# Attention with beacons and a max-out FFN on one core: the steps of the first two batches in another order

## The chip, the core and the metric

The kernel runs on one core of a Trainium2 chip. The core has five engines that run side by side and wait for each other through semaphores: TensorE (PE, matrix products and transposes; its weight loads are shown apart as PEld), VectorE (DVE), ScalarE (ACT), GpSimd (POOL) and SyncE (SP, which here only issues transfers). Sixteen DMA engines move data between the device's memory and the on-chip memory; a request for a transfer stands in the queue of the engine that issues it (SP, ACT or POOL), in that engine's order. The metric is the device time of one execution in microseconds (us).

## What is computed

```python
def _attn_ref(q, k, v, beacon_k, beacon_v):          # B, H, S, Nb, D = 8, 8, 576, 16, 64
    scale = 1.0 / np.sqrt(D)
    k_all = np.concatenate([beacon_k, k], axis=2)
    v_all = np.concatenate([beacon_v, v], axis=2)
    scores = scale * np.matmul(q, k_all.transpose(0, 1, 3, 2))
    causal[:, Nb:] = np.triu(np.ones((S, S), dtype=bool), k=1)
    scores = np.where(causal, -1000000000.0, scores)
    scores = scores - scores.max(-1, keepdims=True)
    a = np.exp(scores)
    a /= a.sum(-1, keepdims=True) + 1e-09
    return np.matmul(a, v_all)

def _moe_ref(x, w1, w2, w3, w_out):                  # x: 4608 x 512, w: 512 x 768, w_out: 768 x 512
    h = np.maximum(np.maximum(x @ w1, x @ w2), x @ w3)
    return h @ w_out
```

All inputs and the output are float32. The heads' attention results of a token, side by side, are a row of x.

## The kernel before

The eight heads of a batch are worked on as four pairs (p is the pair's number over all batches, four to a batch), and two pairs make a quad. For each pair the kernel needs qT and kT, that is q and k with the head dimension on the partitions. In batches 0 to 3 PE turns them (transposes into PSUM, `turn_half` L431, `turn` L387) and another engine copies them out; six buffers of qT and kT go round (L145). In batch 0 a pair is turned in halves of 288 tokens: pair 0 and pair 1 each from their own loads (`load_half` L210, cast to bf16 by `cast_half` L218), the others from quads that a POOL transfer casts on its way (`load_quad` L226). In batch 1 a whole pair is turned at once (`load_whole_quad` L235). Later pairs are loaded in float32 (`load_pair` L192) and cast by an engine (`cast_pair` L254).

The scores of a pair stand in four groups gi (`emit_scores` L506): key tiles by ranges of queries, for both heads. PE writes a group into one of two PSUM tiles named sc (a third, named wide, is added by the step "widen"), and ACT takes the exponential into the pair's SBUF tile at_sb (L532). A mask then zeroes what lies above the diagonal, on POOL (`affine_select`, L551) or on DVE (a product with the triangle tri, L549). "values" (`emit_pv` L571) multiplies a quad's at_sb with ones (the sums) and with v; "invert" (L606) has ACT make the reciprocals, and "multiply" (L618) has DVE write the scaled result into xT, the FFN's input. The v tiles come in float32 and are cast by an engine (`load_first_v` L286, `cast_first_v` L310 in batch 0).

The FFN works on blocks of 512 tokens. Block 0 is cut into 18 half units of 256 tokens (`mm1_halves` L666): for each of the three weights, three units of 8 products each for the low half (kind 0) and three for the high half (kind 1), nine of a kind, weights in order; DVE copies or takes the maximum into hT (L681, L683). Then come units with w_out (`mm2_unit` L685, L690). The weights are fetched by POOL transfers that cast to bf16, two requests for each of the three (`load_w` L323) and one for w_out (`load_w_out` L330).

Nothing schedules this: every engine carries out its instructions in the order in which the program emits them. For batches 0 and 1 that order is a list of named steps, `first_steps` (L892), carried out one after the other (L1100). A step emits instructions on several engines at once. For example ("scores", p, gi, n) emits on PE n filler products (`spare` L479, 128x320 of a constant tile, into the tile that the scores will use) and the scores, and on ACT the exponential. ("half", p, h, bank, engine, idle, idle_q) emits idle_q pairs of small filler transposes (`fill` L407), the turn of q, idle pairs, the turn of k, a copy of q by the named engine and a copy of k by DVE. ("busy", n) emits n fillers. ("keys", p, engine) copies the beacons' keys to kT. Steps whose name begins with "load" only emit requests; where one names an engine, that engine first writes one element of the destination, and the request and all that stands behind it in its queue wait for this. After the list a loop over quads 4 to 15 (L1140 and on) goes on with the later batches, the first of it being one last half unit and the scores of pair 8. The loop is not changed.

```python
    def emit_all():
        for name, *args in first_steps:
            steps[name](*args)
```

Of the kernel before, what the change touches and what calls it, by code (L numbers as in the profile page):

```python
# [16 lines left out]
def kernel(  # L17
# [120 lines left out]
    busy = const.tile([128, 320], BF16, name="busy")  # L138
# [709 lines left out]
    def widen():  # L848
# [43 lines left out]
    first_steps = [  # L892
        ("load half", 0, 0, "sp"),
        ("busy", 17),
        ("identity",),
        ("busy", 8),
        ("triangle",),
        ("load quad half", 1, 0),
        ("load half", 1, 0, "act"),
        ("load half", 0, 1, "act"),  # L900
        ("cast half", 0, 1, "dve"),
        ("load keys 0", "act"),
        ("cast keys 0", "act"),
        ("load half", 1, 1, "sp"),
        ("cast half", 0, 0, "act"),
        ("cast half", 1, 0, "act"),
        ("load v0", 0, "dve"),
        ("half", 0, 0, "ffn", "act", 0, 7),
        ("cast half", 1, 1, "act"),
        ("turn keys 0",),  # L910
        ("load v0", 1, "pool"),
        ("keys", 3, "act"),
        ("load v0", 2),
        ("keys", 1, "act"),
        ("keys", 2, "pool"),
        ("load quad half", 0, 1),
        ("half", 1, 0, "ffn", "act", 2, 9),
        ("scores", 0, 0, 0),
        ("scores", 1, 0, 3),
        ("load w", 0),  # L920
        ("cast v0", 0, "pool"),
        ("half", 3, 0, "ffn", "act", 0, 0),
        ("mask", 0, 0, "dve"),
        ("cast v0", 1, "dve"),
        ("half", 2, 0, "pv", "dve", 4, 0),
        ("cast v0", 2, "act"),
        ("scores", 3, 0, 3),
        ("mask", 1, 0, "pool"),
        ("scores", 2, 0, 6),
        ("values", 0, 0, "pv", 0, 4, 0),  # L930
        ("half", 0, 1, "ffn", "act", 0, 7),
        ("invert",),
        ("load v0", 3, "dve"),
        ("scores", 0, 2, 4),
        ("mask", 3, 0, "dve"),
        ("mask", 2, 0, "dve"),
        ("scores", 0, 3, 0),
        ("multiply",),
        ("values", 1, 0, "ffn", 0, 4, 0),
        ("invert",),  # L940
        ("half", 1, 1, "pv", "act", 0, 0),
        ("multiply",),
        ("scores", 0, 1, 0),
        ("mask", 0, 3, "dve"),
        ("load quad half", 1, 1),
        ("scores", 1, 2, 0),
        ("load keys 1",),
        ("load v0", 4, "dve"),
        ("mask", 0, 1, "pool"),
        ("ffn", "ffn", 0),  # L950
        ("load w", 1),
        ("mask", 1, 2, "dve"),
        ("ffn", "ffn", 0),
        ("mask", 0, 2, "pool"),
        ("scores", 1, 3, 0),
        ("half", 2, 1, "pv", "act", 0, 0),
        ("scores", 1, 1, 0),
        ("ffn", "ffn", 0),
        ("mask", 1, 3, "pool"),
        ("half", 3, 1, "pv", "dve", 0, 0),  # L960
        ("scores", 2, 3, 0),
        ("cast v0", 3),
        ("load quad", 1, 0),
        ("scores", 2, 2, 7),
        ("cast v0", 4),
        ("scores", 3, 2, 0),
        ("mask", 1, 1, "dve"),
        ("cast keys 1", "pool"),
        ("values", 0, 1, "pv", 0, 4, 0),
        ("scores", 3, 3, 0),  # L970
        ("load w", 2),
        ("turn keys 1",),
        ("keys", 4, "act"),
        ("ffn", "ffn", 0),
        ("mask", 3, 3, "pool"),
        ("load v", 1, 0, "pool"),
        ("mask", 2, 3, "pool"),
        ("invert",),
        ("keys", 5, "act"),
        ("scores", 2, 1, 0),  # L980
        ("mask", 2, 2, "pool"),
        ("multiply",),
        ("ffn", "ffn", 0),
        ("mask", 2, 1, "pool"),
        ("mask", 3, 2, "pool"),
        ("ffn", "ffn", 0),
        ("scores", 3, 1, 1),
        ("mask", 3, 1, "dve"),
        ("whole", 4, "ffn", "dve"),
        ("widen",),  # L990
        ("values", 1, 1, "pv", 0, 4, 0),
        ("invert",),
        ("scores", 4, 1, 0),
        ("multiply",),
        ("scores", 4, 2, 1),
        ("whole", 5, "ring", "act"),
        ("ffn", "ring", 1),
        ("mask", 4, 1, "dve"),
        ("ffn", "ring", 1),
        ("scores", 5, 0, 1),  # L1000
        ("scores", 4, 0, 0),
        ("scores", 4, 3, 0),
        ("ffn", "pv", 1),
        ("ffn", "ring", 0),
        ("load pair", 8, "dve"),
        ("ffn", "pv", 1),
        ("scores", 5, 3, 0),
        ("mask", 5, 0, "dve"),
        ("mask", 4, 2, "dve"),
        ("mask", 5, 3, "dve"),  # L1010
        ("load pair", 9, "pool"),
        ("scores", 5, 2, 0),
        ("load quad", 1, 1),
        ("mask", 4, 3, "dve"),
        ("keys", 7, "act"),
        ("scores", 5, 1, 0),
        ("mask", 4, 0, "pool"),
        ("ffn", "pv", 0),
        ("ffn", "ring", 0),
        ("load v", 1, 1),  # L1020
        ("load", 2, "dve"),
        ("whole", 6, "ring", "dve"),
        ("keys", 6, "pool"),
        ("ffn", "pv", 1),
        ("mask", 5, 2, "pool"),
        ("cast v", 1, 0),
        ("scores", 6, 2, 0),
        ("scores", 6, 1, 0),
        ("mask", 5, 1, "pool"),
        ("scores", 6, 0, 0),  # L1030
        ("ffn", "pv", 1),
        ("load", 1),
        ("values", 2, 0, "ring", 0, 4, 0),
        ("invert",),
        ("keys", 9, "act"),
        ("cast pair", 8),
        ("load w_out", "dve"),
        ("whole", 7, "ring"),
        ("mask", 6, 0, "pool"),
        ("ffn", "pv", 1),  # L1040
        ("multiply",),
        ("cast pair", 9),
        ("load", 2, "dve"),
        ("scores", 6, 3, 0),
        ("scores", 7, 2, 0),
# [188 lines left out]
```

## Time and profile before

| | us |
|---|---|
| median of 3 runs | 294.38 (293.03 to 295.4) |
| profiled execution | 294.65 |
| its span | 292.6 |
| PE, PEld busy | 281.3 (96%), 160.1 (55%) |
| DVE, ACT, POOL busy | 169.6 (58%), 150.5 (51%), 115.8 (40%) |

The profile is that of one execution. The span begins before the first instruction and ends with the last; 2.05 us of the execution lie outside it. Times in the profile count from the span's start. PE is busy nearly throughout, but that includes the fillers, and the ends of its matmuls are modelled. What the profile offers beside totals is used below: the timeline (instructions in order, like ones merged), the chain of waits (followed back from the end), the list of who waited for whom, and busy times in windows.

The part of the program that the list makes up takes about the first 58 us. Up to there PE waits as follows (total, times, longest):

| PE operation | waited for | us |
|---|---|---|
| fillers at the start | DVE, constant tile | 1.3 |
| w_out units | DMA of w_out | 0.7 |
| scores | POOL, L551 (see the prediction) | 0.6 |
| half units | DMA of w | 0.6 |
| scores | DVE copy of qT | 0.6 |
| scores | ACT copies of qT | 0.5 and 0.3 |
| values | DVE mask | 0.4 |
| half units | DVE, xT | 0.3 |

### The profile page before, as it was taken

The page shows a single profiled execution, that of the slowest core. Times are in us where ns is not written, and L with a number is a line of the kernel's source. Part 1 is how long each engine was busy: PE and PEld are TensorE (multiplying, and loading weights), DVE is VectorE, ACT ScalarE, POOL GpSimd, SP SyncE. Part 2 cuts the span into 40 slices and gives each one's busy share as a digit, 9 for nine tenths or more (in the row PEclk, how much of TensorE's full clock was granted, in tenths as well). Part 3 has the DMA queues.
Part 4 walks back from the last instruction along what each step waited for, and adds up shares of the span by engine and source line. Part 5 has one row for each costly group of instructions (what it writes and reads, how often), then busy time and mean ns, then how long its engine had stood idle before and what let it go on. Part 6 is the DMA issues. An engine that isn't in the chain of part 4 may idle for free.

```text
span 292.6 us, 8864 instructions
## 1 busy us (share of the span) xinstructions
PE 281.3 (96%) x3714; PEld 160.1 (55%) x3739; DVE 169.6 (58%) x319; ACT 150.5 (51%) x242; POOL 115.8 (40%) x238
## 2 busy tenths in 40 slices
PE   8889999989999999999999999999999999999995
PEld 4656677754454555454545887545454545444442
DVE  1555567837756575566655656565656564474273
ACT  3786576853566676846676256635663552200300
POOL 3618415742546583426454655466323420000000
PEclk9999999999999999999999999999999999999999
DMA  7999979999989999998999899999442003001103
GB/s 131 161 175 185 217 123 225 228 192 261 229 230 256 232 281 270 186 175 263 314 190 181 233 256 268 177 205 214 104 68 98 2 0 137 11 0 74 71 1 143
DMA packets 85111, 49.50 MB, mean 169 GB/s; under 512 B 64208, under 2 KB 79824, under 8 KB 85072
## 3 DMA queue, kind: packets, MB, share of 16 engines
q1 hardware_dynamic: 78864, 43.40, 66.6%
q0 software_dynamic: 5648, 5.21, 11.7%
q8 instruction: 29, 0.48, 0.7%
q10 hardware_dynamic: 560, 0.33, 0.4%
q14 instruction: 10, 0.08, 0.1%
HBM read 35.13 MB, written 14.22 MB: 169 GB/s over the span
## 4 chain that ended last, share of the span: by engine, by line
PE 86%; DMA 7%; POOL 2%; ACT 2%; DVE 1%; issue 1%; POOLq 0%
PE pv L654 21%; PE sc L654 15%; PE wide L654 8%; PE pv L690 6%; PE sc L690 6%; PE sc L517 5%; PE pv L592 4%; DMA w_out_sb<-in_moe_w_out_dram 4%; PE wide L690 3%; PE wide L592 3%; PE sc L592 3%; PE wide L517 3%; DMA w_sb<-in_moe_w_dram 3%; PE pv L481 2%; PE pv L673 1%
## 5 line engine op out<-in xcount | busy, mean ns | idle before, releaser
L532 ACT ACTIVATE at_sb<-sc 128x736 bf16<-128x736 f32 (+5 forms) x91 | 76.5, 867 | 59.3 <-PE sc L517 59.1
L551 POOL TENSOR_SCALAR_AFFINE_SELECT at_sb<-at_sb 128x256 bf16<-128x256 bf16 (+3 forms) x140 | 51.9, 387 | 117.3 <-ACT at_sb L532 117.1
L654 PEld LDWEIGHTS <-w_sb 128*128 128x128 bf16 x648 | 61.1, 98 | 60.4 <-issue 4.7
L654 PE MATMUL pv<-xT,w_sb 128*128 128x512 bf16 (+1 forms) x315 | 65.3, 347 | 0.3
L654 PE MATMUL sc<-xT,w_sb 128*128 128x512 bf16 (+1 forms) x205 | 45.6, 363 | 0.7 <-issue 0.2
L532 ACT ACTIVATE at_sb<-wide 128x736 bf16<-128x736 f32 (+3 forms) x37 | 31.3, 846 | 22.4 <-PE wide L517 22.4
L664 DVE TENSOR_TENSOR hT<-hT,pv 128x512 bf16<-128x512 bf16 x48 | 32.4, 686 | 13.0 <-PE pv L654 13.0
L690 PEld LDWEIGHTS <-hT 128*128 128x128 bf16 x210 | 19.6, 98 | 24.3 <-issue 1.1
L248 POOL CAST p<-st 96x768 bf16<-96x768 f32 x40 | 32.0, 824 | 0.0
L624 DVE TENSOR_TENSOR xT<-pv,recip 128x288 bf16<-128x288 f32 (+2 forms) x48 | 14.2, 350 | 26.7 <-ACT recip L614 26.7
L517 PE MATMUL sc<-qT,kT 64*128 64x288 bf16 (+6 forms) x290 | 27.2, 275 | 2.0 <-POOL at_sb L551 0.6
L664 DVE TENSOR_TENSOR hT<-hT,sc 128x1024 bf16<-128x1024 bf16 (+1 forms) x18 | 19.6, 1098 | 12.7 <-PE sc L654 12.5
L517 PEld LDWEIGHTS <-kT 64*128 64x128 bf16 x400 | 14.9, 94 | 21.8 <-issue 14.7
L592 PEld LDWEIGHTS <-v_sb 128*32 128x32 bf16 (+1 forms) x1408 | 24.7, 96 | 2.6 <-issue 1.3
L654 PE MATMUL wide<-xT,w_sb 128*128 128x512 bf16 (+1 forms) x110 | 24.5, 364 | 0.1
L690 PE MATMUL sc<-w_out_sb,hT 128*128 128x512 bf16 x79 | 19.1, 380 | 1.0 <-DMA w_out_sb<-in_moe_w_out_dram 0.7
L690 PE MATMUL pv<-w_out_sb,hT 128*128 128x512 bf16 x83 | 19.9, 380 | 0.1
L304 POOL CAST v_sb<-st 128x1536 bf16<-128x1536 f32 (+2 forms) x21 | 18.4, 895 | 0.0
L662 DVE CAST hT<-pv 128x512 bf16<-128x512 f32 x20 | 13.7, 688 | 4.8 <-PE pv L654 4.8
L673 PEld LDWEIGHTS <-w_sb 128*128 128x128 bf16 x144 | 13.1, 98 | 3.9 <-issue 1.4
L614 ACT ACTIVATE recip<-lnd 128x288 f32<-128x288 f32 x32 | 14.2, 444 | 1.0
L592 PEld LDWEIGHTS <-ones 128*32 128x32 bf16 (+2 forms) x512 | 11.0, 95 | 6.7 <-issue 4.7
(116 smaller groups left out, 286.3 us busy)
## 6 DMA issues: line engine op xcount, KB each, us to landing
st<-in_q_dram SPq DMA_DIRECT2D x24, 288.0 KB, 5.3
st<-in_k_dram SPq DMA_DIRECT2D x24, 288.0 KB, 5.7
st<-in_v_dram SPq DMA_DIRECT2D x24, 256.0 KB, 5.8
out_dram<-y SPq DMA_DIRECT2D x9, 512.0 KB, 3.3
out_dram<-y SPq DMA_DIRECT2D x17, 256.0 KB, 2.7
w_sb<-in_moe_w_dram POOLq DMA_DIRECT2D x6, 384.0 KB, 7.2
q_dram<-p SPq DMA_DIRECT2D x16, 144.0 KB, 3.1
k_dram<-p SPq DMA_DIRECT2D x16, 144.0 KB, 3.2
```

The lines of the kernel that those rows point to most:

```text
L248: cast(t16.rearrange("p r h d -> p h r d"), st[0:QP, i * NQ2 : (i + 1) * NQ2].rearrange("p (h r d) -> p h r d", h=2, r=QR),)
L304: cast(v_sb[0:n, t:t1].rearrange("p t h d -> p (t h d)"), st[0:n, (t - t_lo) * H * D : (t1 - t_lo) * H * D],)
L517: nc.tensor.matmul(ps[:, e, off : off + q1 - q0], kT[hs, 128 * t : 128 * t + 128], qT[hs, q0:q1], start=True, stop=True, tile_position=(64 ...
L532: nc.scalar.activation(out=both_heads(p, gi), in_=ps[:, :, 0 : g_width(p, gi)], func=AF.Exp, scale=scale)
L551: nc.gpsimd.affine_select(out=view, in_=view, compare_op=ALU.is_ge, fill=0.0, base=x0, pattern=[[0, 2], [1, hi - lo]], channel_multiplier=-1,)
L592: nc.tensor.matmul(ps[bank][32 * j : 32 * j + 32, lo + q0 - qa : lo + qb - qa], lhsT, at_view(PPQ * quad + j // 2, t, j % 2, q0, qb), star ...
L614: nc.scalar.activation(out=recip, in_=lnd, func=AF.Exp, scale=-1.0)
L624: nc.vector.tensor_mul(xT[:, 2 * g + part - 1, c0 + ca : c0 + cb], ps[bank][:, lo : lo + cb - ca], recip[:, ca:cb],)
L654: nc.tensor.matmul(dst[:, o0 : o0 + n], w_in[i][:, ct, 128 * (ft + f) : 128 * (ft + f + 1)], xT[:, ct, x0 : x0 + n], start=(ct == 0), stop ...
L664: nc.vector.tensor_max(h, h, ps)
L673: nc.tensor.matmul(ps[:, f], w_in[i][:, ct, 128 * (ft + f) : 128 * (ft + f + 1)], xT[:, ct, tb * TOKB + lo : tb * TOKB + hi], start=(ct == 0),
L690: nc.tensor.matmul(ps[:, t - tt] if two else ps, hT[:, ft, 128 * t : 128 * (t + 1)], w_out_sb[:, ft, :], start=(ft == 0), stop=(ft == n_ft ...
```

## The change

Only the list `first_steps` is rewritten; it has 174 steps before and after. The number of units, scores, values, turns, masks and requests stays, their order and engines change:

- Fillers: 25 ahead of the first turn become 31, the 26 in the scores' steps become 20, the small pairs 49 instead of 29.
- Pairs 0 to 3 are turned in their first halves (with pairs 1 to 3's q copied by DVE) before any scores; before, scores of pairs 0 and 1 stood between.
- Casts: pair 0's q half from ACT to DVE and its k half from DVE to ACT; v tiles 0 to 4 from POOL, DVE, ACT, POOL, POOL to ACT, DVE, POOL, DVE, POOL; the beacons' keys of batches 1 to 3 from POOL to ACT.
- Masks: 16 on DVE and 16 on POOL become 15 and 17, many on another engine than before. Beacon copies: ACT 6 and POOL 3 become ACT 3, DVE 1, POOL 5.
- Requests: the first weights behind the mask of pair 0 and the first halves' turns, the others' places in POOL's order moved as the diff shows; v of batch 0 early; v of batch 1 later; pair 8 gated by POOL instead of DVE; w_out without its gate.

The diff, cut:

```diff
     first_steps = [
+        ("busy", 10),
+        ("load half", 0, 1, "act"),
+        ("load half", 1, 0, "act"),
         ("load half", 0, 0, "sp"),
-        ("busy", 17),
         ("identity",),
-        ("busy", 8),
+        ("load half", 1, 1, "sp"),
+        ("busy", 21),
+        ("load keys 0", "act"),
+        ("cast half", 0, 0, "dve"),
+        ("load v0", 0, "pool"),
         ("triangle",),
+        ("cast half", 0, 1, "act"),
+        ("cast keys 0", "act"),
         ("load quad half", 1, 0),
-        ("load half", 1, 0, "act"),
-        ("load half", 0, 1, "act"),
-        ("cast half", 0, 1, "dve"),
-        ("load keys 0", "act"),
-        ("cast keys 0", "act"),
-        ("load half", 1, 1, "sp"),
-        ("cast half", 0, 0, "act"),
+        ("load v0", 1, "dve"),
+        ("load v0", 2, "dve"),
         ("cast half", 1, 0, "act"),
-        ("load v0", 0, "dve"),
-        ("half", 0, 0, "ffn", "act", 0, 7),
+        ("half", 0, 0, "ffn", "act", 3, 12),
         ("cast half", 1, 1, "act"),
         ("turn keys 0",),
-        ("load v0", 1, "pool"),
-        ("keys", 3, "act"),
-        ("load v0", 2),
-        ("keys", 1, "act"),
-        ("keys", 2, "pool"),
+        ("cast v0", 0, "act"),
+        ("keys", 2, "dve"),
+        ("keys", 1, "pool"),
         ("load quad half", 0, 1),
-        ("half", 1, 0, "ffn", "act", 2, 9),
-        ("scores", 0, 0, 0),
-        ("scores", 1, 0, 3),
+        ("half", 1, 0, "pv", "dve", 2, 9),
+        ("half", 2, 0, "pv", "dve", 5, 0),
+        ("half", 3, 0, "ffn", "dve", 1, 2),
+        ("scores", 0, 0, 2),
+        ("keys", 3, "pool"),
+        ("load v0", 3, "dve"),
+        ("mask", 0, 0, "pool"),
+        ("cast v0", 1, "dve"),
         ("load w", 0),
-        ("cast v0", 0, "pool"),
-        ("half", 3, 0, "ffn", "act", 0, 0),
-        ("mask", 0, 0, "dve"),
-        ("cast v0", 1, "dve"),
-        ("half", 2, 0, "pv", "dve", 4, 0),
-        ("cast v0", 2, "act"),
-        ("scores", 3, 0, 3),
-        ("mask", 1, 0, "pool"),
-        ("scores", 2, 0, 6),
+        ("cast v0", 2, "pool"),
+        ("scores", 1, 0, 4),
+        ("scores", 2, 0, 0),
+        ("scores", 3, 0, 8),
+        ("mask", 1, 0, "dve"),
         ("values", 0, 0, "pv", 0, 4, 0),
...
```

From there to the first half units with the second weights the two lists read:

| before | after |
|---|---|
| half (0,1), invert, load v 3, scores (0,2), masks (3,0) (2,0) on DVE, scores (0,3), multiply, values (1,0), invert, half (1,1), multiply, scores (0,1), mask (0,3) DVE, load quad half (1,1), scores (1,2), load keys 1, load v 4, mask (0,1) POOL, unit, **load w 1**, mask (1,2) DVE, unit, mask (0,2) POOL, scores (1,3), half (2,1), scores (1,1), unit, mask (1,3) POOL, half (3,1), scores (2,3), cast v 3 POOL, load quad (1,0), scores (2,2) with 7 fillers, cast v 4 POOL, scores (3,2), mask (1,1) DVE, cast keys 1 POOL, values (0,1), scores (3,3), **load w 2**, turn keys 1, keys 4, unit | masks (2,0) DVE (3,0) POOL, invert, half (0,1), multiply, scores (0,2) (0,3), values (1,0), load quad half (1,1), load keys 1, invert, half (1,1), scores (0,1), multiply, scores (1,2), cast keys 1 ACT, load v 4, mask (1,2) POOL, **load w 1**, cast v 3 DVE, mask (0,1) DVE, scores (1,3), unit, unit, half (2,1), scores (1,1), mask (0,3) POOL, unit, load quad (1,0), half (3,1), masks (0,2) (1,3) POOL (1,1) DVE, cast v 4 POOL, scores (2,3) (2,2) with 1 filler, (3,2), values (0,1), scores (3,3), turn keys 1, keys 5 POOL, unit, invert, mask (2,3) POOL, scores (2,1), **load w 2** |

Further on, what the prediction speaks of:

```diff
-        ("load v", 1, 0, "pool"),
...
+        ("mask", 3, 3, "pool"),
+        ("ffn", "ffn", 0),
+        ("mask", 3, 2, "pool"),
+        ("multiply",),
+        ("scores", 3, 1, 0),
+        ("mask", 2, 2, "dve"),
+        ("mask", 2, 1, "pool"),
+        ("keys", 4, "act"),
+        ("ffn", "ring", 0),
         ("mask", 3, 1, "dve"),
-        ("whole", 4, "ffn", "dve"),
+        ("whole", 4, "ffn", "act"),
         ("values", 1, 1, "pv", 0, 4, 0),
...
+        ("ffn", "ring", 1),
+        ("ffn", "ring", 1),
+        ("load v", 1, 0, "pool"),
+        ("scores", 5, 0, 0),
+        ("ffn", "ring", 0),
...
+        ("load pair", 8, "pool"),
...
+        ("load quad", 1, 1),
...
+        ("whole", 6, "ring", "dve"),
...
+        ("ffn", "pv", 1),
+        ("ffn", "ring", 0),
+        ("mask", 5, 2, "pool"),
+        ("scores", 6, 0, 0),
...
+        ("cast v", 1, 0),
...
+        ("whole", 7, "ring", "dve"),
+        ("mask", 5, 1, "dve"),
+        ("values", 2, 0, "ring", 0, 4, 0),
+        ("keys", 9, "pool"),
+        ("invert",),
+        ("scores", 6, 2, 0),
+        ("cast pair", 8),
+        ("load w_out",),
```

Before, the load of pair 8 stood behind a gate on DVE, and the load of w_out behind one as well, after the cast of pair 8 and the values (2,0).

## The prediction

> **What bounds it now.** The list of steps that is reordered runs until the first scores of pair 8. I read the page's slices first (PE at 8 or 9 tenths everywhere), then the timeline for where that stage ends and the first output matmul follows:
>
> ```profile
> 1.33 6.33 PE L481 MATMUL pv<-busy 128*128 128x320 bf16 x25 [1.33 <-DVE busy L139]
> 14.20 0.40 PE L517 MATMUL sc<-qT,kT 64*128 64x288 bf16 x6 [0.61 <-POOL at_sb L551]
> 48.00 0.53 PE L517 MATMUL sc<-qT,kT 64*128 64x464 bf16 x6 [0.56 <-DVE qT L456]
> 52.66 0.37 PE L517 MATMUL sc<-qT,kT 64*128 64x464 bf16 x2 [0.30 <-ACT qT L456]
> 58.40 0.54 PE L517 MATMUL sc<-qT,kT 64*128 64x288 bf16 x8
> 63.18 2.76 PE L690 MATMUL sc<-w_out_sb,hT 128*128 128x512 bf16 x11 [0.73 <-DMA w_out_sb<-in_moe_w_out_dram]
> ```
>
> The columns are start, length, engine, line, tiles, count, and in brackets PE's idle time and its releaser. The stage ends at 58.40. From there PE works towards w_out and stands 0.73 us. The waits of PE behind 65 us sum to 0.2 us, so a slip of the stage reaches the end unless w_out absorbs it. The chain of waits shows what a reordering can touch (start, length, link):
>
> ```profile
> 14.60 1.34 PE pv L592 x44
> ...
> 21.56 0.41 POOL at_sb L551
> 21.96 0.49 POOL w_sb L326
> 22.46 7.48 DMA w_sb<-in_moe_w_dram
> 29.98 0.83 PE fps L673 x6
> ...
> 50.77 12.37 DMA w_out_sb<-in_moe_w_out_dram
> ```
>
> A weight request stands on POOL behind a mask, and its transfer ends a wait of PE; w_out is the second. The windows (PE, PEld, DVE, ACT, POOL busy, granted clock, DMA share, GB/s) show the DMA engines full up to 41 us but for short dips, then a hole:
>
> ```profile
> 38.00:40.00 2.00, 2.00 (x24) 1.57 (x22) 1.75 (x4) 1.06 (x2) 0.00 (x0) 1.00 1.29 208
> 42.00:44.00 2.00, 2.00 (x22) 1.38 (x21) 1.64 (x4) 0.94 (x2) 0.89 (x3) 1.00 0.03 6
> ```
>
> **The change, walked by anchors.** Work of use is the same: 17 FFN units, 32 scores, 6 values, 8 half turns, 6 whole ones, the same requests. Each step below starts at the latest of PE's order and its last input, with durations from the timeline.
>
> *Fillers.* Ahead of the first turn 25 fillers become 31. They start 266 ns apart while PE is slow ((5.58 - 1.33)/16) and 133 ns from 6.83 on; a new bank between the two groups costs 0.24. After: ten until 4.24, ten slow ones to 6.9, eleven fast ones to 8.4. The 12 pairs of small fillers ahead of q (24 at 23 ns, from 14 in 0.32) add 0.55, q's six turns 0.2, 3 more pairs 0.14, k's turns 0.18: pair 0 is turned at 9.45 instead of 8.34, **+1.1**. The earlier loads and casts of pair 0 (landed 3.8 to 5.8, casts 0.36 and 0.51) are hidden under this. The Trainium skill, "TensorE: Matmul & The Clock Gate", Part 1, puts the speed-up some 4 us into sustained work; the trace has it after 5.5 us, with a granted clock of 1.00 in all rows. By the page the fillers would end at 7.6 and 0.8 us of this +1.1 would go.
>
> *Turns ahead of scores.* Pair 1's k cast stands on ACT behind qT's copy: q turned 9.13, copy to 9.6, cast to 10.1, turn to 10.55. DVE now copies qT and kT of pairs 1 to 3, 0.44 to 0.46 each with the next started up to 0.1 before the end: pairs 2 and 3 wait for banks until 11.0 and 11.4, and all are turned at 12.4. Scores of pair 0 start at 12.8 (two fillers), before 9.55. Exp 0 runs 13.2 to 14.25, exp 1 to 15.2 (0.97 apart). Scores 3 write the bank that exp 1 frees, and their eight fillers (1.2) come behind that: 16.45 to 16.8. Values (0, 0) start there against 14.53; POOL's mask 0 (1.29, to 15.55), the first weight requests (1.1) and the v cast (0.63, to 17.3) fit just under their sums part. They end 18.15 against 15.87: **+2.3**. Second turn 0.9, copies, scores (0, 2) and (0, 3), values (1, 0) at 20.1 to 21.5, against 19.51: **+2.0**.
>
> *To the second weights.* Turn of pair 1, scores, exp (0, 1) 22.45 to 23.4, two FFN units 23.7 to 25.45, turn 2, scores, a unit, turn 3, scores (2, 3), (2, 2), (3, 2), values (0, 1) 28.75 to 30.4 against 28.67: **+1.7**; the seven fillers there that became one gave back 0.8. The unit with the second weights is due at 30.9. Its request now follows exp (1, 2) (to 24.1) and mask (1, 2) (0.35): both issued by 25.6, before 21.91 to 23.0. From the start of the first to landing of the second it took 29.94 - 21.91 = 8.03, so 32.5: PE stands 1.6 us, and the unit ends 33.35 against 30.74: **+2.6**. The bounds: the second piece lands 4.7 us after its issue as its sibling did (29.75, no wait, +1.05) or 8.3 (the slowest weight request, +3.4); I take 7.5, the same two pieces back to back.
>
> *To the stage's end.* Scores (2, 1), unit, scores (3, 1), unit, turn 4, values (1, 1): 0.3 + 0.9 + 0.3 + 0.9 + 0.7 + 1.65 = 4.75, so 38.1 against 36.13, **+2.0**; before, a filler and a wait for mask (3, 1), which followed exp at 34.48, took 0.64 more. From there before needs 22.27. After lacks two fillers (0.24 each), and the waits of 0.56 and 0.30 shown above: pair 6 is now turned two units (1.8) ahead of its scores, against 1.5 of copies; pair 7's copies have values, scores and a unit over them. 38.1 + 22.27 - 0.5 - 0.86 = **59.0, +0.6**. Covers to watch: third weights requested at 32.0 against 27.5 (POOL puts them behind beacons and a mask), landing about 38 to 41.7, due 41.45; the second whole quad due at 46.4.
>
> *w_out.* It loses its gate on DVE and follows pair 8's cast on POOL: exp (5, 2) 46.0, mask 0.4, v cast 1.5, pair casts 1.6, issue 49.6, landing 12.4 later at 62.0. PE is there at 59.0 + (62.45 - 58.40) = 63.05: no wait, and the start moves by -0.1. The 0.73 was the cushion; a later slip counts in full. The rest of the redeal (beacon copies 0.2 each, v casts 0.41 to 0.64, one v gate from none to DVE, pair gates between DVE and POOL, the memsets under 0.1) lies on engines idle by half; the gates hold SP's requests behind them, and cost nothing while pairs 8 and 9, asked for at about 37 instead of 43.3, fill the hole in the DMA.
>
> *Masks against casts.* The mean of masks hides a price:
>
> ```profile
> L549 DVE TENSOR_TENSOR at_sb<-at_sb,tri x3: 279/496/782, 11.6 to 12.2; 128x224 bf16<-128x224 bf16 x1, 128x256 bf16<-128x256 bf16 x1, 48x96 bf16<-48x96 bf16 x1
> L549 DVE TENSOR_TENSOR at_sb<-at_sb,tri x6: 194/268/283, 17.3 to 18.2; 128x224 bf16<-128x224 bf16 x2, 128x256 bf16<-128x256 bf16 x2, 48x96 bf16<-48x96 bf16 x2
> L549 DVE TENSOR_TENSOR at_sb<-at_sb,tri x1: 698/698/698, 26.4 to 26.4; 128x256 bf16<-128x256 bf16 x1
> ```
>
> (min/median/max ns, starts.) The same shapes take 0.19 to 0.29 with POOL idle, and up to 0.78 beside POOL's v casts (12.29 to 12.92, 26.33 to 26.95). After, masks (1, 0), (2, 0), (1, 1) on DVE lie beside POOL's masks and both v casts. Each hit is 0.41 (698 - 285) to 0.59 (782 - 195); three are possible on the path (0 to 1.5). I take one, **+0.4**, and 0.3 for the two tight transfers, the middle of 0 and 0.6.
>
> Sum at the first output matmul: -0.1 + 0.4 + 0.3 = +0.6 on the profiled execution's 294.65 (292.6 of span, 2.05 around it), which lies 0.27 over the median 294.38: **295.0**.
>
> **Rivals.**
> A, weights do not bind: the second piece lands as the first did (less is queued ahead, as v and first halves were asked for early), and no mask is hit. Then units run from 30.9, the stage ends at 57.5, PE is at w_out at 61.5 and stands 0.5 there: 63.18 - 62.0 = 1.2 saved, 293.2; if the v and pair casts free w_out earlier too, up to 3. Against it: the same two pieces took 8.03 with little ahead.
> B, slower: POOL's queue starves the DMA. First weights go out 4.4 us later (15.6), the first quad's second halves 5.1, third weights 4.5, each behind a mask that waits for an exp; the engines have little to move from about 7 to 16 us and must make it up. Taken end to end behind 32.5: whole quad 2.6 (29.94 to 32.5), third weights 3.1 (to 35.6), v and second whole quad 7.1 (to 42.7), pair 8 2.8: 48.1 against 46.4 due, 1.7 us of wait; 0.8 more if the second weights take 8.3, and 0.8 at w_out, whose pair cast is late with pair 8: 3.3 above the forecast's -0.1, so **297.9**. It decides once the transfers are over 1 us behind at turn 6. For it: the share above 1.0 from 14 us on. Against: the hole at 42 to 44 pays 2.7.
> C, the lock between DVE and POOL: all three hits, 1.5 instead of 0.4: 296.1, and over 1% slower only if the later masks beside pair casts join in. The Trainium skill, "SBUF — State Buffer", Who interferes with whom, says a DVE operation with two SBUF inputs and a POOL one that reads SBUF exclude each other; the rows above agree. By that rule every overlap pays in full.
>
> **The numbers.** Forecast 0.43, A 0.25, B 0.20, C 0.12. One per cent (2.9 us, little more than the 2.4 us between the three runs of before) is what can be told from no change. Faster by more: 0.10 of A and 0.02 of the forecast (fast clock early as well): 0.12. Slower: 0.15 of B, 0.04 of C, 0.06 of the forecast for a wait I have not seen: 0.25. Same: 0.63. Range: down to A with no transfer in the way, 292.2; up to B and one more hit, 298.6.
>
> **What would show it.** Pair 0 turned at 9.45; values (0, 0) ending near 18.1; a wait of PE for w_sb near 31 of 1.6 us; no wait for w_out; scores of pair 8 at 59 to 59.5. A stage end under 58 is A; waits for whole quads or third weights at 40 to 47 are B; DVE masks of 0.7 us ahead of PE's sums are C. I am wrong at the root if time appears behind 65 us, where nothing is reordered.

## The result, and the profile after

| kernel | us: median (lowest to highest, runs) | ratio to before, 95% interval |
|---|---|---|
| before | 293.78 (292.85 to 295.4, 20) | |
| after | 295.95 (294.18 to 297.99, 20) | 1.0076 [1.0058, 1.0094] |

The change costs 2.2 us, 0.8%. This is inside one per cent and inside the range, 0.95 over the forecast of 295.0. The ratios here and in the table of the experiments leave out single slow runs, over 1.5% above the fastest of the same kernel (three of e5's, one each of e3's and e8's, and one of 473 us of the kernel before); the medians in the tables count all runs. The profiled execution of after took 297.39 (span 295.7) and lies 1.4 over its median: it is one of 7 in 20 whose mean granted clock was 0.988 to 0.994. These average 297.2, the other thirteen 295.5, which is still 1.7 over before. All 17 runs of before beside the first four experiments had 0.999 or 1.0; of the 29 beside the next four, two had 0.993 and 0.994.

The timeline of after (start, length, engine, line, tiles, count; in brackets PE's idle time and its releaser):

```profile
1.34 5.92 PE L481 MATMUL pv<-busy 128*128 128x320 bf16 x31 [1.34 <-DVE busy L139]
...
15.69 0.97 PE L592 MATMUL pv<-at_sb,v_sb 128*32 128x288 bf16 x32
...
18.72 0.97 PE L592 MATMUL fps<-at_sb,v_sb 128*32 128x288 bf16 x32
...
29.69 0.39 PE L673 MATMUL fps<-xT,w_sb 128*128 128x256 bf16 x2 [0.56 <-DMA w_sb<-in_moe_w_dram]
31.52 1.46 PE L673 MATMUL fps<-xT,w_sb 128*128 128x256 bf16 x6 [1.44 <-DMA w_sb<-in_moe_w_dram]
...
33.44 1.75 PE L673 MATMUL fps<-xT,w_sb 128*128 128x256 bf16 x8
...
55.76 0.32 PE L517 MATMUL wide<-qT,kT 64*128 64x336 bf16 x2 [1.14 <-DVE xT L624]
...
61.43 0.33 PE L517 MATMUL wide<-qT,kT 64*128 64x288 bf16 x4
...
66.14 0.20 PE L592 MATMUL wide<-at_sb,v_sb 80*32 80x80 bf16 x1 [1.68 <-issue]
66.26 2.76 PE L690 MATMUL sc<-w_out_sb,hT 128*128 128x512 bf16 x11
```

Values (1, 0) end at 19.69, only 0.2 later than before (19.51). PE then stands 0.56 and 1.44 us for the second weights where it stood 0.59, and the rows behind that wait are slow: six products in 1.46 us where before has 0.83, eight in 1.75 where a unit takes 1.05. The windows say why (PE, PEld, DVE, ACT, POOL busy, granted clock, DMA share, GB/s):

```profile
28.00:30.00 2.00, 1.44 (x60) 1.03 (x48) 0.00 (x0) 1.15 (x4) 0.01 (x1) 1.00 1.18 182
30.00:32.00 2.00, 0.56 (x4) 0.36 (x4) 0.00 (x0) 0.69 (x2) 2.00 (x6) 0.88 1.07 162
32.00:34.00 2.00, 2.00 (x12) 0.92 (x11) 0.69 (x1) 0.46 (x1) 0.15 (x1) 0.50 0.96 169
34.00:36.00 2.00, 2.00 (x17) 1.21 (x15) 0.77 (x2) 0.99 (x2) 1.13 (x4) 0.77 0.98 184
```

The granted clock is 0.50 from 31.5 to 34.9 (by the rows 0.48, 2.00 and 0.92 us): in this execution a wait of two microseconds is paid for again in half clock. Ahead of the wait, the chain of waits has the request at the place that the prediction gave it:

```profile
22.57 0.51 POOL w_sb L326
23.09 8.38 DMA w_sb<-in_moe_w_dram
31.52 1.46 PE fps L673 x6
...
64.45 1.68 issue
```

The waits of 0.56 and 0.30 us for copies of pairs 6 and 7 are gone, as credited, and w_out (issued 51.50, landed 63.5) is in before PE wants it. In their place stand 1.14 us at 55.76 and 1.68 us of "issue" at 64.45. The scores of pair 8 start at 61.43 against 58.40, the first output product at 66.26 against 63.18, and from there on the spans differ by the same 3.1.

What the 1.14 us is, DVE's timeline shows:

```profile
53.45 0.74 DVE L456 COPY qT<-sc 128x576 bf16<-128x576 bf16 x1
54.12 0.79 DVE L549 TENSOR_TENSOR at_sb<-at_sb,tri 80x160 bf16<-80x160 bf16 x1
54.83 0.87 DVE L624 TENSOR_TENSOR xT<-wide,recip 128x288 bf16<-128x288 f32 x3
```

The multiply that frees the tile wide stands behind two copies and mask (5, 1). That mask, 80x160, took 0.23 in the profile before (at 39.32) and takes 0.79 here, beside POOL's cast of pair 9 (53.22, 1.59 for two).

### The profile page after: what moved, and what is told of

It reads as the page before. It is cut to its first block, busy times and chain, and to the rows that moved or that the text cites. A ratio compares the mean times of both kernels' runs of the same rounds, so it can differ in the third digit from the quotient of the medians.

```text
span 295.7 us, 8937 instructions
## 1 busy us (share of the span) xinstructions
PE 282.6 (96%) x3754; PEld 160.2 (54%) x3779; DVE 170.7 (58%) x316; ACT 150.7 (51%) x238; POOL 116.4 (39%) x243
## 4 chain that ended last, share of the span: by engine, by line
PE 90%; DMA 3%; DVE 2%; ACT 2%; issue 2%; POOL 0%
PE pv L654 21%; PE sc L654 16%; PE wide L654 6%; PE pv L690 6%; PE sc L517 6%; PE sc L690 5%; PE pv L592 4%; PE sc L592 4%; PE wide L690 4%; PE wide L592 3%; PE wide L517 3%; DMA w_sb<-in_moe_w_dram 3%; PE pv L481 2%; PE pv L673 2%; PE sc L673 2%
## 5 line engine op out<-in xcount | busy, mean ns | idle before, releaser
L532 ACT ACTIVATE at_sb<-sc 128x992 bf16<-128x992 f32 (+5 forms) x91 | 75.8, 858 | 51.1 <-PE sc L517 51.0
L551 POOL TENSOR_SCALAR_AFFINE_SELECT at_sb<-at_sb 128x256 bf16<-128x256 bf16 (+3 forms) x143 | 52.5, 384 | 118.3 <-ACT at_sb L532 118.2
L654 PE MATMUL sc<-xT,w_sb 128*128 128x512 bf16 (+1 forms) x224 | 49.0, 364 | 0.5 <-issue 0.2
L532 ACT ACTIVATE at_sb<-wide 128x992 bf16<-128x992 f32 (+3 forms) x37 | 32.1, 868 | 32.9 <-PE wide L517 32.9
L664 DVE TENSOR_TENSOR hT<-hT,sc 128x1024 bf16<-128x1024 bf16 (+1 forms) x19 | 22.1, 1163 | 15.0 <-PE sc L654 14.6
L517 PE MATMUL sc<-qT,kT 64*128 64x288 bf16 (+6 forms) x284 | 28.3, 278 | 0.6 <-ACT at_sb L532 0.3
L654 PE MATMUL wide<-xT,w_sb 128*128 128x512 bf16 (+1 forms) x91 | 20.7, 361 | 0.3
L690 PE MATMUL sc<-w_out_sb,hT 128*128 128x512 bf16 x69 | 16.6, 379 | 0.2
L702 DVE COPY y<-pv 128x512 f32<-128x512 f32 x14 | 9.7, 692 | 8.4 <-PE pv L690 6.7
```

Source lines behind the costliest of these rows:

```text
L517: nc.tensor.matmul(ps[:, e, off : off + q1 - q0], kT[hs, 128 * t : 128 * t + 128], qT[hs, q0:q1], start=True, stop=True, tile_position=(64 ...
L532: nc.scalar.activation(out=both_heads(p, gi), in_=ps[:, :, 0 : g_width(p, gi)], func=AF.Exp, scale=scale)
L551: nc.gpsimd.affine_select(out=view, in_=view, compare_op=ALU.is_ge, fill=0.0, base=x0, pattern=[[0, 2], [1, hi - lo]], channel_multiplier=-1,)
L654: nc.tensor.matmul(dst[:, o0 : o0 + n], w_in[i][:, ct, 128 * (ft + f) : 128 * (ft + f + 1)], xT[:, ct, x0 : x0 + n], start=(ct == 0), stop ...
L664: nc.vector.tensor_max(h, h, ps)
L690: nc.tensor.matmul(ps[:, t - tt] if two else ps, hT[:, ft, 128 * t : 128 * (t + 1)], w_out_sb[:, ft, :], start=(ft == 0), stop=(ft == n_ft ...
```

## The experiments

Ratios are to the kernel before, run beside them.

| run | us: median (lowest to highest, runs) | ratio, 95% interval |
|---|---|---|
| e1_w1_early | 301.27 (299.28 to 302.53, 6) | 1.0243 [1.0205, 1.0280] |
| e2_rows | 294.73 (293.93 to 296.69, 12) | 1.0037 [1.0017, 1.0058] |
| e3_mask51 | 297.34 (294.74 to 299.66, 6) | 1.0099 [1.0060, 1.0138] |
| e4_warm | 297.42 (295.10 to 299.20, 6) | 1.0120 [1.0076, 1.0164] |
| e5_start_fill | 295.73 (292.59 to 299.31, 12) | 1.0038 [1.0003, 1.0073] |
| e6_first_part | 294.71 (292.90 to 296.11, 12) | 1.0015 [0.9986, 1.0043] |
| e7_second_part | 294.63 (292.81 to 296.70, 12) | 1.0027 [0.9998, 1.0057] |
| e8_wout_early | 298.47 (295.51 to 300.79, 6) | 1.0128 [1.0073, 1.0184] |
| e9_w_first | 299.89 (297.88 to 301.51, 6) | 1.0198 [1.0164, 1.0231] |
| e10_wout_free | 293.42 (292.16 to 295.41, 12) | 0.9983 [0.9962, 1.0003] |
| e11_pair_early | 293.60 (292.59 to 294.69, 12) | 0.9986 [0.9969, 1.0003] |
| e12_turns_early | 292.77 (291.74 to 295.15, 12) | 0.9966 [0.9943, 0.9988] |

### Ask for the weights earlier: e1_w1_early and e9_w_first

```diff
 e1: the second weights earlier
         ("load quad half", 1, 1),
+        ("load w", 1),
...
-        ("load w", 1),
 e9: neither request behind a mask
+        ("load w", 0),
         ("mask", 0, 0, "pool"),
...
-        ("load w", 0),
...
-        ("mask", 1, 2, "pool"),
         ("load w", 1),
+        ("mask", 1, 2, "pool"),
```

> The changed kernel with one step moved: the requests for the second weights go out right after the second halves of pairs 2 and 3, no longer behind mask (1, 2), in a stretch where POOL idled 3.5 us. Theory (the late second weights cost PE 0.56 + 1.44 us of wait against 0.6 before, and the wait lets PE's clock fall to half, 1.6 us more, in some executions): no wait for w_sb, clock 1.00 in all executions, 2 to 2.5 us less than the changed kernel's 295.95, so about 0 to 0.3 below before. Rival (the DMA engines are the bound, the order of requests only shifts whose wait it is): the wait comes back at the first weights, at a quad or at the third weights, and the time falls by less than 0.7.

> The changed kernel with the first weights requested ahead of mask (0, 0) and the second ahead of mask (1, 2), both on POOL, so that neither request waits for an exponential. Theory (rival B of the prediction: requests held behind masks leave the DMA engines short of work early, and every later landing slips): first weights go out by 12.5 us against 13.7, the second ones land by 30.6 against 31.5, no wait for them above 0.7 us, no rows at half clock in the profile; ratio 1.002 to 1.005. Rival (as in e1_w1_early: the total of bytes binds, and a v tile or w_out is late instead): ratio 1.006 or more, with a wait for v or w_out of 0.8 us or more.

Both theories fell, and both rivals were right, by more than expected. In neither profile does PE wait for weights. It waits for v tile 4 instead. PE and POOL of e9 (timeline):

```profile
20.19 1.11 POOL L326 DMA_DIRECT2D w_sb<-in_moe_w_dram  x2
...
32.58 0.61 POOL L316 CAST v_sb<-st 80x512 bf16<-80x512 f32 x1 [6.31 <-DMA st<-in_v_dram]
...
33.24 0.73 PE L592 MATMUL pv<-at_sb,v_sb 80*32 80x80 bf16 x40 [3.52 <-POOL v_sb L316]
```

In after, the request for v tile 4 goes out at 21.73 and the weights at 22.52; the tile is being cast at 25.94, and the weights land at 31.47. In e9 the weights go out at 20.19 and v at 23.20, and the cast of v starts at 32.58, 9.4 us later. The two transfers together take until about 32 either way, with the DMA engines full; what is asked for second comes last. v is due first (values (0, 1) end at 28.8, the unit with the second weights is due at 29), so the order of the list is the better one. In e1 the wait for v is 2.9 us, another of 0.85 us for a quad's k lies ahead of it. For rival B of the prediction, which has the masks ahead of the weights starve the DMA engines, this means that asking ahead of the masks is no cure: the weights then come in time, and v is late by more than that gains. In e9 the clock behind the wait is at half again (0.79 mean from 32 to 40).

### The wait with the word "issue": e2_rows and e4_warm

```diff
 e2: 50 PE instructions fewer, as much filler time
-        ("busy", 21),
+        ("busy", 26),
...
-        ("half", 0, 0, "ffn", "act", 3, 12),
+        ("half", 0, 0, "ffn", "act", 0, 0),
 e4: 14 large fillers ahead of the unit that waits for the second weights
         ("keys", 5, "pool"),
+        ("warm", 14),
         ("ffn", "ffn", 0),
```

> The changed kernel with the 15 pairs of small fillers ahead of and within pair 0's first turn (30 at 23 ns, 0.69 us) exchanged for 5 large ones (0.67 us): PE's program is 50 instructions shorter from there on, and nothing else changes. Theory (the 1.68 us in which PE stood at 64.45 for nothing that the profile shows is a wait for the next 256 of its instructions, since the 0.56 us of before lies exactly 256 instructions earlier in PE's program): the same wait moves 50 instructions further, out of the values into the w_out units, where PE uses its instructions slower, and shrinks or goes: 0.5 to 1.7 us less. Rival (the wait belongs to the work: a tile's release or w_out landing): it stays at the last product of the values, and the time with it.

> The changed kernel with 14 large fillers (1.9 us) added ahead of the unit that waits for the second weights, so that PE is busy in the wait. Theory (after the wait PE runs at half clock for about 3.5 us in some executions, which makes the difference between the 297 to 298 us and the 294 to 296 us executions): the clock is 1.00 in all executions, none is above 296.5, and the median falls by 0.3 to 0.7. Rival (the slow executions have another cause): executions of 297 and more are as frequent as in the changed kernel (7 of 20), and the median is the same or up to 0.5 higher.

PE's instructions (weight loads, products, waits) can be counted in the program's own order. The 0.56 us of before stand ahead of number 1986, the 1.68 us of after ahead of number 2242: 256 apart. In e4, with 28 instructions more ahead, the wait must move 14 products up if it belongs to the number and not to the product:

```profile
62.24 1.04 PE L592 MATMUL wide<-at_sb,v_sb 128*32 128x288 bf16 x41
63.83 0.35 PE L592 MATMUL wide<-at_sb,v_sb 128*32 128x96 bf16 x15 [0.54 <-issue]
64.10 2.76 PE L690 MATMUL sc<-w_out_sb,hT 128*128 128x512 bf16 x11
```

15 products are left where after had one. In e2, with 50 fewer, number 2242 falls among the output products, and no wait is seen there; 0.24 us stand at number 1986. So PE's program comes in blocks of 256 instructions, and PE stands at a block's edge when the block is not in. The transfers themselves are in the profile's DMA view (of after, for 63 to 64 us; transfers, MB, share of 16 engines):

```profile
q8 instruction: 1, 0.02, 8.9%
```

29 of these in the execution move 0.48 MB, 16 KB each. In seven profiles (before, after, e1, e7, e9, e10, e12) the transfer starts 2.3 to 3.0 us before PE goes on, and takes 0.9 to 1.4 us; in after it starts at 63.1 and PE goes on at 66.14. What sets the moment of its start was not found. That a values step suffers most fits its pace: 152 instructions in 1.6 us, where an FFN unit has 16 in 1.05. The Trainium skill, "Runtime: NRT & Kernel Launch", Instruction fetch mechanics, states blocks of 16 KiB, 256 instructions, and that crossing an edge is mostly hidden. The traces agree with the 256. Of the 29 transfers of an execution at most three are followed by a wait of PE (none in e6's profile), so most are hidden here too; those that are not cost 0.2 to 2.5 us each.

As to time, e2 is 1.2 us under after. How much of that is the block's edge was not shown: w_out, in at 64.97, then holds PE 1.0 us, so not all of the 1.68 came home, and only one of e2's twelve executions has a mean clock under 0.995, against seven of 20. The executions without it average 294.9, against 295.5. e4 takes away both the wait for weights and the half clock in its profiled execution (295.25, the second fastest of six, against 297.39 for that of after), yet its median is 1.5 over after's. Its theory fell: four of the six are above 296.5, and two still have a mean clock of 0.994. Fillers of 1.9 us are spent in every execution, the wait they fill is not there in every one; whether this is the reason was not shown.

### The mask behind the copies: e3_mask51

```diff
-        ("mask", 5, 1, "dve"),
+        ("mask", 5, 1, "pool"),
```

> The changed kernel with mask (5, 1) on POOL, as before, instead of DVE. Theory (PE's 1.14 us at 55.76 is for the tile wide, which DVE's multiply frees, and the multiply stood behind this mask, which took 0.79 beside POOL's pair cast instead of 0.23): the wait falls to 0.4 to 0.6 and the time by 0.5 to 0.7. Rival (DVE's copies of pair 7 and the reciprocal set it, or POOL's casts behind the mask come late instead): the time moves by under 0.3.

The wait for the tile wide fell from 1.14 to 0.4 us, as the theory said, in part because PE comes to it later here (the multiply starts at 54.99, in after at 54.83). The time did not follow. In the profile three masks of DVE take 2.65 us together from 50.49 (in after the same three take 0.98 from 51.28), and between 50 and 56 us PE waits 0.83 us for hT, 0.65 for a mask and 0.80 for qT, none of which after has. Whether the moved mask brings these hits about was not shown: another mask takes 1.29 us at 47.87, beside a v cast (47.55), before the moved one has run on POOL (48.96), and DVE is 1.8 us earlier there than in after, whose profile has the half clock.

### Which part of the list holds the loss: e5_start_fill, e6_first_part, e7_second_part

```diff
 e5: the fillers of the start as before
-        ("busy", 21),
+        ("busy", 15),
...
-        ("half", 0, 0, "ffn", "act", 3, 12),
+        ("half", 0, 0, "ffn", "act", 0, 7),
 e6: steps 1 to 47 of after (through values (1, 0)), then steps 48 on of before
 e7: steps 1 to 47 of before, then steps 48 on of after
```

> The changed kernel with the earlier kernel's starting fillers: 25 large ones instead of 31 ahead of the first turn, and no small fill of 3 times 12 inside the first q turn (0 times 7 instead); 44 rows of TensorE fewer than the changed kernel. Theory (the start slip passes through, and the issue stall of 1.7 us moves out of the values product into the first output units): pair 0 is turned before 8.0 us, values (0, 0) end by 16.2, no issue wait above 0.8 us between 60 and 66 us, time 293.5 (ratio 0.995 to 1.001). Rival (landings set the end: second weights at 31, w_out at 64 to 65, whatever TensorE does before): the wait for w_out is 1 us or more and the time is that of e2_rows, 294.7 (ratio 1.002 to 1.005).

> The first 47 steps of the changed kernel (through values (1, 0)) and the rest of the earlier one. Theory (most of the loss arises after values (1, 0): the second weights' wait with its half clock, a later wait of 1.1 us for a bank, the issue stall): values (1, 0) end within 0.5 of 19.6, and the time is at most 0.7 over the kernel before (ratio 1.000 to 1.0025). Rival (the start costs what the prediction gave it, 2.0 us at values (1, 0), and keeps it): ratio 1.005 or more.

> The first 47 steps of the earlier kernel and the rest of the changed one. Theory (the loss arises after values (1, 0)): a wait for the second weights of 1 us or more near 30 us with rows at half clock behind it, a stage end 2 us or more over 58.4, ratio 1.004 to 1.008. Rival (the start holds it): ratio 0.999 to 1.002. If the two parts add up, the excess of this run and of e6_first_part sum to about 2.2 us; if they do not, the loss lies in how they meet.

Excess over before in ratios: 0.0015 and 0.0027 for the parts, 0.0076 for the whole. With intervals of 0.003 to each side this neither shows nor excludes that they add up. Both expectations were met in part. e6 has the small ratio of the theory, but its profiled execution has the place of the prediction:

```profile
1.34 7.36 PE L481 MATMUL pv<-busy 128*128 128x320 bf16 x31 [1.34 <-DVE busy L139]
...
17.13 0.97 PE L592 MATMUL pv<-at_sb,v_sb 128*32 128x288 bf16 x32
...
20.16 0.97 PE L592 MATMUL fps<-at_sb,v_sb 128*32 128x288 bf16 x32
```

Values (0, 0) end at 18.10 (predicted 18.15), values (1, 0) at 21.13 (predicted 21.5). The instructions up to there are those of after, which had them at 16.66 and 19.69. The difference is the fillers: 31 took 5.92 in after and 7.36 in e6 (6.64, 7.02, 7.18 and 7.39 in e4, e3, e1 and e9), 25 took 5.24 to 6.33 in before, e5, e7, e8 and e10 to e12. The same work differs by up to 1.5 us with the moment at which PE's spacing goes from 266 to 133 ns, and that moment varies between executions of the same instructions. In e6 1.4 us of it reach the scores of pair 8 (59.83) and the first output product (64.56).

e7 missed the wait that its theory named; there is none for weights over 0.2 us. It has another edge instead, at number 1218, which is 1986 less three times 256:

```profile
35.90 0.36 PE L392 MATMUL wide<-ident,whole 96*64 96x96 bf16 x7
38.11 0.57 PE L392 MATMUL wide<-ident,whole 96*64 96x96 bf16 x17 [1.85 <-issue]
...
38.00:40.00 2.00, 1.89 (x24) 1.45 (x25) 0.90 (x2) 0.49 (x1) 0.00 (x0) 0.65 1.27 191
40.00:42.00 2.00, 2.00 (x11) 1.23 (x9) 0.69 (x1) 0.15 (x1) 0.00 (x0) 0.50 1.22 235
```

The half clock follows a wait for instructions as it follows one for data. Scores of pair 8 are at 61.22, w_out waits nothing, and the first output product starts at 64.80. e5 keeps the order of after and starts as its theory said (pair 0 turned at 7.25, values (0, 0) end at 15.92, no issue wait over 0.2 between 60 and 66 us). The rival's wait for w_out is not there; PE stands 1.24 us for the third weights at 40.20. In this profiled execution the loss of the stage is gone, and other time appears where nothing is reordered:

```profile
62.72 2.76 PE L690 MATMUL sc<-w_out_sb,hT 128*128 128x512 bf16 x12
...
113.80 0.81 PE L654 MATMUL wide<-xT,w_sb 128*128 128x512 bf16 x3 [0.87 <-issue]
...
143.62 2.76 PE L654 MATMUL sc<-xT,w_sb 128*128 128x512 bf16 x12 [0.47 <-issue]
```

The first output product starts 0.46 us ahead of that of before and 3.5 ahead of that of after. From there to the end of the span e5 takes 231.1 us; before, after and nine of the other runs take 229.4 (e2 230.0, e8 230.4). The two waits are 1.3 of the 1.7 us, and they stand five and eight times 256 instructions behind number 2242, 3.3 and 2.5 us after the start of a transfer of instructions: fillers taken away at the start move the edges of all later blocks, in code that the list does not touch. The ratio, 1.0038, is in the rival's range and about half of after's excess, but the median of all twelve runs lies only 0.2 under that of after. With runs from 292.6 to 299.3 the share of the fillers in the loss is not settled.

### w_out: e8_wout_early and e10_wout_free

```diff
 e8: on top of e5
+        ("load w_out",),
         ("cast v", 1, 0),
...
-        ("load w_out",),
 e10: the kernel before, its gate on DVE taken away
-        ("load w_out", "dve"),
+        ("load w_out",),
```

> e5_start_fill with the request for w_out ahead of the v cast of batch 1 on POOL, some 4 us earlier. Theory (w_out is late only because it is asked for late): issue at 46 to 48 us, landing by 60.5, no wait for it, time 0.5 to 1.0 under e5_start_fill. Rival (the DMA engines are full, and what goes earlier makes another late): w_out takes longer than 13 us, or a wait of 0.5 or more for a pair or v appears between 50 and 62 us, and the time is that of e5_start_fill within 0.3.

> The kernel before with one part of the change alone: the request for w_out has no gate on DVE. Theory (the gate holds POOL 1.83 us, and w_out's landing ends the last wait ahead of the output product): issue at 48.9 to 49.2 instead of 50.77, landing by 62, the wait of 0.73 us falls under 0.2, ratio 0.9970 to 0.9985. Rival (DMA full from 46 us: what w_out gains, pairs or v lose): ratio 0.999 to 1.004, with a new wait of 0.4 us or more between 50 and 60 us.

e8: w_out goes out at 44.89 and is in at 53.7, far ahead of its use, and the v tiles of batch 1 pay: POOL idles 3.61 us for their transfer, PE stands 0.62 and 0.75 us for the casts. The rival's waits came. The time did not stay within 0.3 of e5's: it is 2.7 us over it (1.0128), and the profile, of the fastest of the six executions (295.51), does not show why.

e10: as its theory said, w_out goes out at 48.9, lands at 61.0, and its wait is gone. The ratio is in the range given, though its interval reaches 1.0003. Part of the gain is lost at the edge at number 1986, where PE waits longer, 1.03 us for 0.56: the first output product starts at 63.05, only 0.13 ahead of the kernel before.

### What of the change is good: e11_pair_early and e12_turns_early

```diff
 e11: e10, and pair 8 into the hole of the DMA engines
+        ("load pair", 8, "dve"),
         ("mask", 4, 1, "dve"),
...
-        ("load pair", 8, "dve"),
 e12: e11, and two turns earlier
+        ("whole", 6, "ring", "dve"),
         ("ffn", "ring", 0),
...
-        ("whole", 6, "ring", "dve"),
...
+        ("whole", 7, "ring"),
         ("values", 2, 0, "ring", 0, 4, 0),
...
-        ("whole", 7, "ring"),
```

> e10_wout_free with pair 8 asked for five steps earlier, ahead of mask (4, 1), to fill the hole that the DMA engines of the kernel before show from 41 to 44.5 us. Theory (bytes moved into the hole bring all later landings forward): pair 8 issued by 40.5 instead of 43.3, DMA share above 0.5 at 42 to 44, w_out landed by 61, ratio 0.995 to 0.998, the lowest of all kernels here. Rival (TensorE's own order sets the end once w_out is in): ratio that of e10_wout_free within 0.001.

> e11_pair_early with two more pieces of the change: the whole turn of pair 6 one FFN unit earlier (two units ahead of its scores) and that of pair 7 ahead of values (2, 0). Theory (with w_out in by 60.3 in e11_pair_early, TensorE's order sets the end, and the waits of 0.56 and 0.30 us for copies of qT go, as the prediction credited them): neither wait is seen, the first output product starts 0.6 to 0.9 us earlier, ratio 0.994 to 0.997, both under e11_pair_early and with an interval below 1. Rival (the block of instructions that PE waits for at row 1986, 1.03 us in the two runs before, is fetched late whatever PE does, and absorbs it): that wait grows to 1.5 us or more, ratio 0.998 to 1.001.

e11 fills the hole (the second line was 0.03 and 6 GB/s before):

```profile
40.00:42.00 2.00, 2.00 (x21) 1.80 (x19) 1.01 (x2) 1.75 (x3) 0.80 (x3) 1.00 1.14 269
42.00:44.00 2.00, 2.00 (x22) 1.38 (x21) 1.82 (x7) 1.19 (x2) 0.08 (x1) 1.00 1.07 256
```

w_out lands at 60.3, and the time is that of e10: the rival was right, since PE comes to w_out only at 62.07. So PE's own order is what is left, and e12 takes up the prediction's credit for the two waits:

```profile
47.17 0.53 PE L517 MATMUL sc<-qT,kT 64*128 64x464 bf16 x6
...
51.37 0.36 PE L517 MATMUL sc<-qT,kT 64*128 64x464 bf16 x2
...
52.87 0.39 PE L517 MATMUL sc<-qT,kT 64*128 64x288 bf16 x4 [0.39 <-DVE xT L624]
...
59.80 0.30 PE L592 MATMUL pv<-at_sb,v_sb 128*32 128x80 bf16 x12 [0.51 <-issue]
...
61.56 2.76 PE L690 MATMUL sc<-w_out_sb,hT 128*128 128x512 bf16 x11
```

Neither wait is left, a new one of 0.39 gives part back. The wait at number 1986 did not grow, so the rival is out; the first output product starts 0.5 us earlier than in e11, a little less than the theory's 0.6. The ratio 0.9966 is the one of all twelve whose interval lies under 1, but this interval overlaps those of e10 and e11, so what the turns add to these is not shown by the times. Ungated w_out, an earlier pair 8 and earlier turns are all parts of the change; on the order of before they are worth 0.9 us (292.77 against 293.70 beside it).

## Why the prediction was right, and where its steps were not

The number held. The sum that led to it was off by 2.5 us in the profiled execution (first output product +3.1 instead of +0.6) and by 1.6 in the medians (+2.2 instead of +0.6). That it held is in part luck. The forecast was only 0.95 off because the median of three runs that it stood on, 294.38, lay 0.6 over that of twenty; and in the profiled execution PE was 1.8 us ahead of the sum at values (1, 0), which hid part of the 4.3 us that it lost to the sum from there to the first output product.

- **Fillers, "pair 0 is turned at 9.45 instead of 8.34, +1.1"**: 8.2 in the profile of after, 9.64 in that of e6. The step took the moment of the fast clock, 6.8 us in one execution, for a constant. By the spacing of the fillers it lies between some 4 and 7 us. The rule of the Trainium skill that is set against it there, with 7.6 for the fillers' end, came nearer for after (7.26) and further off for e6 (8.70). The Trainium skill, "TensorE: Matmul & The Clock Gate", Part 1, also says that the window runs free of the kernel; the spread of 4 to 7 us bears this out.
- **Values (0, 0) at 18.15, (1, 0) at 21.5**: 16.66 and 19.69 in after, 18.10 and 21.13 in e6. The order's price was read rightly for a late fast clock; before loses less with a late one, since its first turn waits for a cast anyway (0.25 us at 7.31 in e7).
- **The second weights, "PE stands 1.6 us, and the unit ends 33.35"**: 2.0 us, and 32.98. The transfer took 8.38 from its second request, at the upper of the two bounds (8.3); the landing (31.47) was 1.0 us earlier than reckoned and PE 1.6, hence the longer wait. Rival A is out.
- **The steps that failed: the 4.75 from the unit to values (1, 1), and "From there before needs 22.27", to 59.0.** The 4.75 were 6.0 (32.91 to 38.95): the products behind the wait were priced at full clock. At half clock they cost 0.63 in the rest of the unit and 0.9 in the scores and the unit after it. The 20.9 that the prediction made of the 22.27 were 22.5 (38.95 to 61.43), with the 1.14 us for the tile wide as the largest part. The prediction says nothing of what the wait itself would do to the clock; but as the thirteen executions with a mean clock over 0.995 are still 1.7 us over before, the half clock is not the main term of the median.
- **The credits 0.56 and 0.30**: right, in after as in e12, where they were taken alone.
- **"I take one [lock], +0.4"**: the early masks on DVE took 2.04 us for six without PE waiting for them. The hit that counted was one that C put at the end of its sentence, "the later masks beside pair casts": 0.79 instead of 0.23, in front of a multiply, 1.14 us of wait. In e3 the wait falls when the mask goes, while other masks beside casts are slow. C's mechanism was right, its place and price were not.
- **"No wait" for w_out, "the start moves by -0.1"**: no wait, as said, though the landing is 63.5 and not 62.0. The 0.73 us so saved went to the block's edge, 1.68 instead of 0.56. The 0.56 was in the profile of before, as an "issue" wait of values; the prediction passed over it, and so did not ask where the edge would fall after 79 more PE instructions.
- **B**: no wait for third weights, whole quads or pairs is in the profile of after; and e9, which takes two of the gates away, is slower. For after it is out; in e5, whose PE is earlier, its wait for third weights is there (1.24 us).

Still open: how the loss of 2.2 us in the median divides between the block's edge, the wait for the tile wide, the second weights and the half clock (the parts' intervals are too wide, and by the mean clock only seven of 20 executions have the half clock, which makes about 0.6 of the 2.2 us by which the means differ, 296.1 against 293.9), and what starts a block's transfer.

## What to carry to other kernels

Price a wait of PE of some two microseconds with what the clock does behind it, not only with its length. When a reordering moves requests, ask which of two transfers in a full stretch is due first; an earlier request for one can be a later landing of the other (e1, e8 and e9 are 1.3 to 2.4% over before, 0.9 to 1.7% over the kernels that they were made from). Where PE's instructions come in blocks, a filler more or less also moves the edges of the blocks behind it (e4, e5). Take a large reorder apart and try its pieces on the old order: here three pieces gain 0.3% and the whole loses 0.8%.

## What was not expected of the hardware

- The same fillers differ by 1.1 to 1.5 us between the profiled executions, by when PE's clock becomes fast (25 of them in 5.24 to 6.33 us, 31 in 5.92 to 7.39). The profile's granted clock reads 1.00 all along; only the spacing shows it.
- Behind waits of 1.85 to 3.5 us the granted clock fell to 0.50 for 3.4 us (after from 31.5, e7 from 38.6, e1 from 34.1, e9 from 34.6); after a single wait of 1.68 (after at 64.45) and one of 1.24 (e5 at 38.96) it stayed at 1.00. By the clock records of these four traces each of these falls comes 8 or 10 steps of 3.41 us after the first entry, and in the step ahead of it PE is idle 0.54 to 0.81 of the time; the wait of 1.68 lies across the edge of two steps and takes at most 0.35 of one. That half a step is the limit was not shown: two steps with 0.53 and 0.54 (e1 from 68.3, e3 from 64.5) have no fall behind them. The Trainium skill, "TensorE: Matmul & The Clock Gate", Part 1, has PE cold after an idle window of about 3.4 us; here less idle time than that was enough.
- PE stood 0.2 to 2.5 us at some of the edges between blocks of 256 of its instructions (numbers 1218, 1986 and 2242, in e5 two more), and the place moves with each instruction added or removed ahead of it.
